# Routing operands in PSUM, late token tiles away from the gather buffer, and the gate computation behind the first split tokens

## The chip, the cores and the metric

The kernel runs on one core of one Trainium2 chip. The metric is the device time of one execution in microseconds (us): the median of three runs of the kernel before is 753.27 us (752.43 to 753.68). A core has five engines that run their own instruction streams: TensorE (PE, products and transposes), VectorE (DVE), ScalarE (ACT), GpSimd (POOL) and SyncE (SP, which starts most transfers). Operands lie in the on-chip memory SBUF; products are written to PSUM, from which DVE and ACT can read and to which they can write.

## The reference

Three layers follow each other on 2304 tokens of 512 numbers (4 batches x 576 positions, 8 heads x 64):

```
kv  = einsum('bhsd,bhse->bhde', k, v)            # attention without softmax
out = einsum('bhsd,bhde->bhse', q, kv)
x   = out / sqrt(mean(out*out) + 1e-6) * g_norm  # norm per token and head

xn, en = x / (|x| + 1e-6), emb / (|emb| + 1e-6)
logits = xn @ en.T / tau                         # 8 experts
expert_idx = argmax(logits);  gate = softmax(logits)[expert_idx]
out[mask]  = gate * (relu(x[mask] @ w1[e]) @ w2[e])   # w1 512x1024, w2 1024x512

h   = x @ w_in;  g = softplus(h)                 # 512 -> 2048
out = g @ w_out                                  # 2048 -> 512
```

## The kernel before

The program has three stages. The head (to about 100 us) computes attention, the norm and the routing, for 18 tiles of 128 tokens. From then on PE works on the experts, one after the other by size ("rank" 0 is the largest), with weights split into two parts of lower precision (wh and wl, as the tokens are into xh and xl), so that one product becomes three (L856 to L858). Then comes the last layer.

In the head, a tile goes through these steps: PE forms the attention output o; ACT squares it (sq, L367) and copies it (cp, L374); DVE sums the squares (ss, L377); for a pair of tiles ACT takes a logarithm and an exponential (rs, L381 and L382) and DVE does a Newton step of three instructions (L151 to L155), which gives rinv; DVE multiplies the logit columns by it (lt, L389) and sums them (lg, L397); POOL multiplies the whole tile by rinv (xa, L403), which a DMA writes to xd in DRAM; and DVE or POOL multiplies xa by g_norm (xo, L416), whose squared norm ACT takes (nn, L419, into ssx). Only the gate needs that norm, the choice of the expert does not.

The tokens are routed in three groups of 6 tiles. For a group DVE finds the best expert (top1, L432 to L442: mx, eq, vm, oh_all), PE counts slots (L451 to L456), DVE forms code, ci, pm and the one-hot tables sel and chk in `early` (L459 to L472), tgb_all (L480), and PE sums them into a token table (L489). DVE counts tokens per expert (acc, L503). After the last group, ranks() sorts the experts by their count (key, cmp, rank, perm, pe, rk_e, L515 to L533) and indices() writes rk_idx (L539 to L547), the rows of xd that each expert wants.

What runs when in the head is decided by a list scheduler: each step has engines, a cost and its predecessors, and the step that can start first with the longest path behind it is issued next; an xo may go to POOL or DVE. Tiles of memory lie in pools: the tile xgt of gathered tokens lies where a head pool was, over xa tiles that were allocated at its start.

Behind the head the code is in written order (L1234 and below). gather() starts POOL's indirect DMAs from xd by rk_idx (L1046), load_w brings weights into st, split_rank makes wh on ACT (CAST, L862) and wl on the named engine (st minus wh, L864); first_transposes turns the gathered tokens on PE (L1076), then ACT makes xh (L1080) and DVE xl (L1084). gates() takes the norm of all tokens (inv_norm: n_x, n_r, L161 to L176), zt = logits minus their maximum (L732), times the norm (L734), exponential on ACT (L736), sum and reciprocal (L739 to L743), then splits the gate in three parts gp (cast and subtract, L747 to L751); each goes into a table tgb (L762), and PE sums these with 18 small products (L766), which stand in PE's program behind the first 36 products of expert 0.

Of the kernel before, what the change touches and what calls it, by code (L numbers as in the profile page):

```python
# [25 lines left out]
def attention_moe_mlp(tc, q, k, v, g_norm, emb, tau, w1, w2, w_in, w_out, out, caps=CAPS):  # L26
# [107 lines left out]
    chk_all = early[:, 64 * NT:76 * NT].bitcast(BF16).rearrange("p (t n) -> p t n", n=3 * E)  # L134
    gate_row, ga_row, rf_row = (early[:, 76 * NT + 384 * i:76 * NT + 384 * i + 384] for i in range(3))
# [13 lines left out]
    def newton(out_, x, r0, r2, half=-0.5):  # L149

        nc.vector.tensor_tensor(out=r2, in0=r0, in1=r0, op=ALU.mult)  # L151
# [34 lines left out]
    with ExitStack() as hs:  # L186
# [147 lines left out]
        xa_t = {i: tp.tile([128, DM], F32, name=f"xa{i}") for i in [*range(7, NT), *range(7)]}  # L334
        xo_t = [tp.tile([128, DM], F32, name=f"xo{i}") for i in range(NXO)]
        ss_t, r0_t, r2_t, rinv_t = ([tp.tile([128, 2, H], F32, name=f"{nm}{i}") for i in range(NSS)] for nm in ("ss", "r0", "r2", "rinv"))
# [77 lines left out]

        def st_xo(t, eng):
            {"G": nc.gpsimd, "D": nc.vector}[eng].tensor_tensor(out=xo_t[t % NXO], in0=xa_t[t], in1=g_rep.rearrange("p h d -> p (h d)"), op=ALU.mult)  # L416

        def st_n(t):
            nc.scalar.activation(out=junk, in_=xo_t[t % NXO], func=AF.Square, accum_out=ssx[:, t:t + 1])  # L419
# [25 lines left out]
        def slots(g):  # L445
# [19 lines left out]
            pm = tp.tile([128, 2, T], I32, name=f"pm{g}")  # L465
# [13 lines left out]
            for u in range(2):  # L479
                nc.vector.tensor_tensor(out=tgb_all[:, u, a:z, :], in0=chk, in1=tok[:, u, a:z].unsqueeze(2).to_broadcast([128, T, 3 * E]), op=ALU.mult)  # L480
                yield

        def tokens(g):
# [7 lines left out]
            if g:  # L491
                nc.vector.tensor_tensor(out=tab, in0=p, in1=tab, op=ALU.add)
            else:
                nc.vector.tensor_copy(tab, p)
# [903 lines left out]
```

## Time and profile before

| | |
|---|---|
| median of 3 runs | 753.27 us (752.43 to 753.68) |
| profiled execution | 752.81 us |
| its span in the profile | 751.0 us |
| mean granted clock of PE | 0.988 of full speed |
| busy: PE, DVE, ACT, POOL | 716.1, 521.9, 408.0, 257.3 us |

The profile is one execution. Times in the rows are microseconds from the start of the span. [...] PE is nearly full from about 100 us to the end; the head is what leaves it waiting.

### The profile page before, as it was taken

Reading aid. Unit: us, or ns where it says so; the run is one execution under the profiler, and the core shown is the slowest. Engines: PE = TensorE matmul, PEld = TensorE weight load, DVE = VectorE, ACT = ScalarE, POOL = GpSimd, SP = SyncE. Lnnn points to the kernel's source line nnn. Section 1 sums busy time; section 2 is a strip of 40 time slices with the busy share of each in tenths; the row PEclk is TensorE's granted clock in tenths of the full one; section 3 lists DMA queues with packets and bytes.
Section 4 is the critical chain, followed back from the end, with each engine's and each line's share of the span. In section 5 each row is a group of like instructions: output and inputs, shape, how many; then the busy total and the mean of one; then the engine's idle time right before and its main releaser. Section 6 shows DMA issues by size and latency. Waiting matters only on the chain.

```text
span 751.0 us, 11433 instructions
## 1 busy us (share of the span) xinstructions
PE 716.1 (95%) x4180; PEld 623.9 (83%) x4180; DVE 521.9 (69%) x944; ACT 408.0 (54%) x753; POOL 257.3 (34%) x190
## 2 busy tenths in 40 slices
PE   9999489999999999998999999999999999999996
PEld 5878279989999999997888878888788878888895
DVE  4588995988688788897787755656555656556564
ACT  2658467646556566554665544445444454345554
POOL 4223456776786877672463020000100020000201
PEclk9999789999999999999999999999999999999999
DMA  9994389898888989831221010000100010000100
GB/s 239 277 265 149 123 277 351 261 324 253 286 280 272 318 282 299 299 96 40 74 84 30 0 57 1 0 1 1 56 1 1 0 43 15 1 1 0 57 1 32
DMA packets 71073, 96.67 MB, mean 129 GB/s; under 512 B 13012, under 2 KB 45804, under 8 KB 71010
## 3 DMA queue, kind: packets, MB, share of 16 engines
q1 hardware_dynamic: 67490, 86.02, 37.3%
q0 software_dynamic: 3344, 9.80, 3.6%
q8 instruction: 35, 0.57, 0.3%
q14 instruction: 28, 0.23, 0.1%
q10 hardware_dynamic: 176, 0.05, 0.0%
HBM read 78.01 MB, written 17.84 MB: 128 GB/s over the span
## 4 chain that ended last, share of the span: by engine, by line
issue 44%; PE 38%; DVE 8%; DMA 4%; ACT 2%; POOL 1%; SPq 1%; ACTq 0%; DVEq 0%; POOLq 0%
PE acc_t L856 9%; PE acc_t L857 9%; PE acc_t L858 9%; DMA out_dram<-orow,idx 2%; PE tp_t L1063 1%; PE misc L301 1%; DMA vr<-in_v_dram 1%; PE tp_t L857 1%; PE tp_t L858 1%; PE tp_t L856 1%; PE acc_t L967 1%; PE acc_t L966 1%; PE acc_t L965 1%; POOL out_dram L972 1%; DVE xs L874 1%
## 5 line engine op out<-in xcount | busy, mean ns | idle before, releaser
L864 POOL TENSOR_TENSOR wl<-st,wh 128x1024 fp32r<-128x1024 f32 x66 | 158.9, 2410 | 71.2 <-ACT wh L862 64.2
L972 POOL DMA_INDIRECT out_dram<-orow,idx x18 | 18.6, 1035 | 324.6 <-ACT orow L971 321.9
L930 ACT ACTIVATE e<-tp_t 128x512 f32<-128x512 f32 (+1 forms) x77 | 42.8, 556 | 131.8 <-PE tp_t L858 131.7
L932 DVE TENSOR_SCALAR u<-e 128x512 f32<-128x512 f32 (+1 forms) x78 | 31.1, 399 | 116.7 <-ACT e L931 116.6
L862 ACT CAST wh<-st 128x1024 fp32r<-128x1024 f32 x72 | 75.2, 1047 | 47.5 <-POOL wl L864 19.7
L856 PE MATMUL acc_t<-hh,wh 128*128 128x368 f32 (+7 forms) x256 | 81.2, 317 | 1.2 <-DVE hl L1213 1.2
L856 PE MATMUL acc_t<-xh,wh 128*128 128x368 f32 (+7 forms) x256 | 79.4, 310 | 0.4 <-ACT x L1230 0.3
L857 PE MATMUL acc_t<-xl,wh 128*128 128x368 f32 (+7 forms) x256 | 79.0, 309 | 0.0
L858 PE MATMUL acc_t<-xh,wl 128*128 128x368 f32 (+7 forms) x256 | 78.9, 308 | 0.0
L858 PE MATMUL acc_t<-hh,wl 128*128 128x368 f32 (+7 forms) x256 | 78.0, 305 | 0.0
L857 PE MATMUL acc_t<-hl,wh 128*128 128x368 f32 (+7 forms) x256 | 78.0, 305 | 0.0
L949 DVE TENSOR_TENSOR gl<-u,gh 128x512 fp32r<-128x512 f32 (+1 forms) x78 | 58.0, 743 | 17.8 <-ACT gh L947 17.8
L938 ACT ACTIVATE u<-u 128x512 f32<-128x512 f32 (+1 forms) x78 | 46.1, 591 | 43.7 <-DVE e L934 43.7
L965 PE MATMUL acc_t<-wh,gh 128*128 128x512 f32 x144 | 56.6, 393 | 5.9 <-ACT gh L947 5.9
L857 PE MATMUL tp_t<-xs,wh 128*128 128x512 f32 (+1 forms) x160 | 59.0, 369 | 0.6 <-DVE xs L874 0.6
L858 PE MATMUL tp_t<-xs,wl 128*128 128x512 f32 (+1 forms) x160 | 58.8, 368 | 0.0
L856 PE MATMUL tp_t<-xs,wh 128*128 128x512 f32 (+1 forms) x160 | 58.8, 368 | 0.0
L967 PE MATMUL acc_t<-wh,gl 128*128 128x512 f32 x144 | 56.5, 392 | 1.3 <-DVE gl L949 1.3
L858 PE MATMUL tp_t<-xs,wl_b 128*128 128x512 f32 (+1 forms) x156 | 57.7, 370 | 0.0
L857 PE MATMUL tp_t<-xs,wh_b 128*128 128x512 f32 (+1 forms) x156 | 57.7, 370 | 0.0
L856 PE MATMUL tp_t<-xs,wh_b 128*128 128x512 f32 (+1 forms) x156 | 57.7, 370 | 0.0
L965 PE MATMUL acc_t<-wh_b,gh 128*128 128x512 f32 x144 | 56.2, 390 | 0.1
(254 smaller groups left out, 1812.0 us busy)
## 6 DMA issues: line engine op xcount, KB each, us to landing
st<-in_moe_w_dram SPq DMA_DIRECT2D x64, 512.0 KB
raw<-in_moe_w_in_dram SPq DMA_DIRECT2D x16, 512.0 KB
raw<-in_moe_w_out_dram SPq DMA_DIRECT2D x16, 512.0 KB
wd<-pre_p SPq DMA_DIRECT2D x32, 256.0 KB
q<-in_q_dram SPq DMA_DIRECT2D x8, 512.0 KB
xd<-xa SPq DMA_DIRECT2D x16, 256.0 KB
st<-wd SPq DMA_DIRECT2D x8, 512.0 KB
raw<-wd SPq DMA_DIRECT2D x8, 512.0 KB
```

What stands on the lines that cost most here:

```text
L856: nc.tensor.matmul(ps_, wh, xh, start=start, stop=False)
L857: nc.tensor.matmul(ps_, wh, xl, start=False, stop=False)
L858: nc.tensor.matmul(ps_, wl, xh, start=False, stop=stop)
L862: nc.scalar.copy(h, raw)
L864: eng.tensor_tensor(out=l, in0=raw, in1=h.bitcast(F32), op=ALU.subtract)
L930: nc.scalar.activation(out=e, in_=h, func=AF.Abs)
L932: nc.vector.tensor_scalar(out=u, in0=e, scalar1=1.0, scalar2=None, op0=ALU.add)
L938: nc.scalar.activation(out=u, in_=u, func=AF.Ln)
L949: nc.vector.tensor_tensor(out=gl, in0=u, in1=gh.bitcast(F32), op=ALU.subtract)
L965: nc.tensor.matmul(mt[b][t_], gh[:, cs_], wh[:, f % 2, :], start=f == 0, stop=False)
L967: nc.tensor.matmul(mt[b][t_], gl[:, cs_], wh[:, f % 2, :], start=False, stop=f == NF - 1)
L972: nc.gpsimd.indirect_dma_start(out=rows_out[i], out_offset=bass.IndirectOffsetOnAxis(ap=idx2[:, i:i + 1], axis=0), in_=o, in_offset=None)
```

## The change

It has three parts. First, the xa of tiles 13 to 17 are allocated ahead of the others, so that the gathered tokens of the first expert lie over xa of tiles 0 to 3. The xo of tiles 10 to 12 are given to POOL, behind its last xa, and those of 13 to 17 to DVE, behind the indices; the last three are kept in `early`. Second, operands of the routing of groups 1 and 2 (mx, eq, pm, key, rank, copies of io8 and tok, the table's last sum) and of the last three Newton steps lie in the PSUM tile misc; key is computed twice, and rs of the late pairs has a second exponential, so that one copy lies in SBUF and one in PSUM. Third, behind the head: zt is formed ahead of the offsets, wl of the first weight piece goes to DVE and of the second to POOL, and gates() stands as a whole behind the transposes and the second weight piece, with the norms of tiles 15 to 17 just ahead of it.

```diff
+    NX0, NX1, NX2 = NT - 8, NT - 5, NT - 3
+    late_xo = [early[:, 76 * NT + 1152 + DM * i:76 * NT + 1152 + DM * i + DM] for i in range(NT - NX2)]
...
-        xa_t = {i: tp.tile([128, DM], F32, name=f"xa{i}") for i in [*range(7, NT), *range(7)]}
+        xa_t = {i: tp.tile([128, DM], F32, name=f"xa{i}") for i in [*range(NX1, NT), *range(NX1)]}
...
-            r0 = r0_t[p % NSS]
+            r0 = r0_t[(p % NSS, "late") if p >= NP1 else p % NSS]
             nc.scalar.activation(out=r0, in_=ss_t[p % NSS], func=AF.Ln)
+            if p >= NP1:
+                nc.scalar.activation(out=r0_t[p % NSS], in_=r0, func=AF.Exp, scale=-0.5, bias=eps)
             nc.scalar.activation(out=r0, in_=r0, func=AF.Exp, scale=-0.5, bias=eps)
...
-            yield from newton(rinv_t[i], ss_t[i], r0_t[i], r2_t[i], -0.5 / D)
+            u = (i, "late") if p >= NP1 else i
+            yield from newton(rinv_t[i], ss_t[i], r0_t[i], r2_t[u], -0.5 / D, r0_t[u])
...
+        def in_misc(*shape, dt=F32):
+            n = int(np.prod(shape))
+            m_at[0] += n
+            tl = misc_t[:, m_at[0] - n:m_at[0]]
+            tl = tl if dt == F32 else tl.bitcast(dt)
+            return tl if len(shape) == 1 else tl.rearrange("p (a b) -> p a b", b=shape[1])
+        NP1 = NT // 2 - 3
+        for i in range(NP1, NT // 2):
+            r0_t[i % NSS, "late"], r2_t[i % NSS, "late"] = in_misc(2, H), in_misc(2, H)
+        def xo_place(t):
+            return late_xo[t - NX2] if t >= NX2 else xo_t[t % NXO]
...
+        tab_l, key, rank_l, io8_l = in_misc(E, 3), in_misc(E), in_misc(E), in_misc(E)
+        tok_l = in_misc(2, TG)
+        mx_l, eq_l = {g: in_misc(TG) for g in range(1, NG)}, in_misc(TG, E)
+        pm_l = in_misc(2, TG, dt=I32)
...
-            mx = mx_all[:, a:z]
+            mx = mx_l[g][:, 0:T] if g else mx_all[:, a:z]
...
-            eq = tp.tile([128, T, E], F32, name=f"eq{g}")
+            eq = eq_l[:, 0:T, :] if g else tp.tile([128, T, E], F32, name=f"eq{g}")
...
-            cnt = misc_t[:, 0:E]
+            cnt = qp_t[1][:, 0, 0:E]
...
-            key = tp.tile([128, E], F32, name="key")
-            nc.vector.scalar_tensor_tensor(out=key, in0=cnt, scalar=float(E), in1=first, op0=ALU.mult, op1=ALU.add)
+            key_s = tp.tile([128, E], F32, name="key")
+            for k_ in (key, key_s):
+                nc.vector.scalar_tensor_tensor(out=k_, in0=cnt, scalar=float(E), in1=first, op0=ALU.mult, op1=ALU.add)
...
+        def st_late():
+            nc.vector.tensor_copy(io8_l, io8)
+            nc.vector.tensor_copy(tok_l, tok[:, :, groups[-1][0]:NT])
...
+                for u in range(NX1, NT):
+                    step(("xo", u), "D", 560, lambda u=u: st_xo(u, "D"), ("idx", 1), ("nn", u - NXO))
+                    if u < NX2:
+                        step(("nn", u), "A", 613, lambda u=u: st_n(u), ("xo", u))
...
-                    step(("xo", u), "GD", (1225, 560), lambda eng, u=u: st_xo(u, eng), ("xa", u), ("nn", u - NXO))
-                    step(("nn", u), "A", 613, lambda u=u: st_n(u), ("xo", u))
+                    if u < NX0:
+                        step(("xo", u), "GD", (1225, 560), lambda eng, u=u: st_xo(u, eng), ("xa", u), ("nn", u - NXO))
+                        step(("nn", u), "A", 613, lambda u=u: st_n(u), ("xo", u))
...
+                if t == NT - 1:
+                    for u in range(NX0, NX1):
+                        step(("xo", u), "G", 1225, lambda u=u: st_xo(u, "G"), ("xa", NT - 1), ("nn", u - NXO))
+                        step(("nn", u), "A", 613, lambda u=u: st_n(u), ("xo", u))
...
             rn = yield from inv_norm(const, ssx, [128, NT], "n")
-            zt = const.tile([128, NT, E], F32, name="zt")
-            nc.vector.tensor_tensor(out=zt, in0=lg_all, in1=mx_all.unsqueeze(2).to_broadcast([128, NT, E]), op=ALU.subtract)
-            yield
             nc.vector.tensor_tensor(out=zt, in0=zt, in1=rn.unsqueeze(2).to_broadcast([128, NT, E]), op=ALU.mult)
             yield
...
+        zt = const.tile([128, NT, E], F32, name="zt")
+        for g, (a, z) in enumerate(groups):
+            mx = mx_l[g][:, 0:z - a] if g else mx_all[:, a:z]
+            nc.vector.tensor_tensor(out=zt[:, a:z, :], in0=lg_all[:, a:z, :], in1=mx.unsqueeze(2).to_broadcast([128, z - a, E]), op=ALU.subtract)
...
-    gts = gates()
-    for _ in range(5):
-        next(gts)
+    split_rank(0, 0, nc.vector)
+    load_w(1, 0)
     fill(tp_tile(), 18)
-    split_rank(0, 0, nc.gpsimd)
-    load_w(1, 0)
     next(pre)
-    for _ in range(5):
-        next(gts)
     first_transposes()
-    split_rank(0, 1, nc.vector)
+    split_rank(0, 1, nc.gpsimd)
     load_w(1, 1)
-    for _ in gts:
+    for u in range(NX2, NT):
+        nc.scalar.activation(out=late_xo[u - NX2], in_=late_xo[u - NX2], func=AF.Square, accum_out=ssx[:, u:u + 1])
+    for _ in gates():
         pass
     split_rank(0, 2, nc.gpsimd)
     load_w(1, 2)
```

In the same way the other operands named above are replaced by their places in misc (tab by tab_l, rank by rank_l, tok by tok_l in the last group).

The next rows are POOL's program from its last xa to the first weights: xa are token tiles, xo those times g_norm, xgt the gathered tokens. Before:

```order
L403 TENSOR_TENSOR xa_278<-oc_268,rinv_307 128x512
L403 TENSOR_TENSOR xa_279<-oc_269,rinv_308 128x512
L403 TENSOR_TENSOR xa_280<-oc_269,rinv_308 128x512
L1046 DMA xgt<-xd,rk_idx 128x512 x2
L1046 DMA xgt<-xd,rk_idx 112x512
L864 TENSOR_TENSOR wl_1186<-st_1130,wh_1184 128x1024
L864 TENSOR_TENSOR wl_1263<-st_1144,wh_1261 128x1024
```

and after the change:

```order
L408 TENSOR_TENSOR xa_273<-oc_269,rinv_308 128x512
L408 TENSOR_TENSOR xa_274<-oc_269,rinv_308 128x512
L438 TENSOR_TENSOR xo_289<-xa_285,g_rep 128x512
L438 TENSOR_TENSOR xo_290<-xa_286,g_rep 128x512
L438 TENSOR_TENSOR xo_291<-xa_287,g_rep 128x512
L1089 DMA xgt<-xd,rk_idx 128x512 x2
L1089 DMA xgt<-xd,rk_idx 112x512
L907 TENSOR_TENSOR wl_1234<-st_1143,wh_1232 128x1024
L907 TENSOR_TENSOR wl_1266<-st_1146,wh_1264 128x1024
```

Three xo stand between the last xa and the gathers, and the first wl product is that of the second weight piece.

ACT's program from its last norm before the expert weights (junk, ssx) to the third weight piece (wh); n_r is the inverse norm, zt the exponential of the gates. Before:

```order
L419 ACTIVATE junk,ssx<-xo_296 128x512
L164 ACTIVATE n_r_1158<-n_x 128x18
L165 ACTIVATE n_r_1158<-n_r_1158 128x18
L862 CAST wh_1184<-st_1130 128x1024
L1080 ACTIVATE xh<-acc_t,gcol 128x256 x3
L1080 ACTIVATE xh<-acc_t,gcol 128x112 x2
L1080 ACTIVATE xh<-acc_t,gcol 128x256
L1080 ACTIVATE xh<-tp_t,gcol 128x112 x2
L862 CAST wh_1245<-st_1141 128x1024
L736 ACTIVATE zt<-zt 128x144
L862 CAST wh_1261<-st_1144 128x1024
```

and after the change:

```order
L441 ACTIVATE junk,ssx<-xo_291 128x512
L905 CAST wh_1158<-st_1132 128x1024
L1123 ACTIVATE xh<-acc_t,gcol 128x256 x3
L1123 ACTIVATE xh<-acc_t,gcol 128x112 x2
L1123 ACTIVATE xh<-acc_t,gcol 128x256
L1123 ACTIVATE xh<-tp_t,gcol 128x112 x2
L905 CAST wh_1232<-st_1143 128x1024
L1293 ACTIVATE early,ssx<-early 128x512 x3
L166 ACTIVATE n_r_1243<-n_x 128x18
L167 ACTIVATE n_r_1243<-n_r_1243 128x18
L775 ACTIVATE zt<-zt 128x144
L905 CAST wh_1264<-st_1146 128x1024
```

Three norms (junk is not used there, the square goes back into `early`), n_r and zt stand between the second and the third weight piece.

DVE's program from the sum of all norms (n_x) on, xl being the lower part of the gathered tokens. Before:

```order
L161 TENSOR_SCALAR n_x<-ssx 128x18
L151 TENSOR_TENSOR n_r_1161<-n_r_1158 128x18
L153 SCALAR_TENSOR_TENSOR n_r_1161<-n_r_1161,n_x 128x18
L155 SCALAR_TENSOR_TENSOR n_r_1158<-n_r_1161,n_r_1158 128x18
L169 TENSOR_TENSOR n_r_1158<-n_r_1158,n_x 128x18
L171 TENSOR_SCALAR n_r_1158<-n_r_1158 128x18
L176 RECIPROCAL n_r_1158<-n_r_1158 128x18
L732 TENSOR_TENSOR zt<-lg_all,mx_all 128x144
L734 TENSOR_TENSOR zt<-zt,n_r_1158 128x144
L1084 SCALAR_TENSOR_TENSOR xl<-acc_t,gcol,xh 128x256 x2
L1084 SCALAR_TENSOR_TENSOR xl<-acc_t,gcol,xh 128x112
L1084 SCALAR_TENSOR_TENSOR xl<-acc_t,gcol,xh 128x256
```

and after the change, with the last xl first:

```order
L1127 SCALAR_TENSOR_TENSOR xl<-tp_t,gcol,xh 128x112 x2
L163 TENSOR_SCALAR n_x<-ssx 128x18
L153 TENSOR_TENSOR n_r_1246<-n_r_1243 128x18
L155 SCALAR_TENSOR_TENSOR n_r_1246<-n_r_1246,n_x 128x18
L157 SCALAR_TENSOR_TENSOR n_r_1243<-n_r_1246,n_r_1243 128x18
L171 TENSOR_TENSOR n_r_1243<-n_r_1243,n_x 128x18
L173 TENSOR_SCALAR n_r_1243<-n_r_1243 128x18
L178 RECIPROCAL n_r_1243<-n_r_1243 128x18
L773 TENSOR_TENSOR zt<-zt,n_r_1243 128x144
L778 TENSOR_REDUCE gate_all<-zt 128x18
L780 TENSOR_SCALAR gate_all<-gate_all 128x18
L782 RECIPROCAL gate_all<-gate_all 128x18
```

The norm and zt were ahead of the xl and are behind them, followed without a break by the sum of the gates.

## Rows read from the trace of the kernel before

**Rows 1.** The page, part 1: busy time of each engine, share of the span, instructions.
```profile
PE 716.1 (95%) x4180; PEld 623.9 (83%) x4180; DVE 521.9 (69%) x944; ACT 408.0 (54%) x753; POOL 257.3 (34%) x190
```

**Rows 2.** The chain of waits, 80 to 111 us: start, us, what.
```profile
100.13 0.65 PE acc_t L856
...
104.11 0.31 PE acc_t L858
...
107.19 0.17 PE acc_t L858
...
108.87 0.72 PE tp_t L766 x18
```

**Rows 3.** Timeline of DVE, 69 to 90.5: start, us, engine, line, operation, out<-in.
```profile
70.95 1.07 DVE L442 TENSOR_TENSOR oh_all<-eq,vm 128x48 bf16<-128x48 f32 x1
...
80.02 0.69 DVE L377 TENSOR_REDUCE ss<-sqb 128x8 f32<-128x520 f32 x1
...
80.70 1.43 DVE L416 TENSOR_TENSOR xo<-xa,g_rep 128x512 f32<-128x512 f32 x1
...
83.96 0.97 DVE L437 TENSOR_TENSOR eq<-eq,first 128x48 f32<-128x48 f32 x1
...
85.19 0.21 DVE L442 TENSOR_TENSOR oh_all<-eq,vm 128x48 bf16<-128x48 f32 x1
...
86.11 0.21 DVE L459 TENSOR_TENSOR code<-rt,oh_all 128x48 f32<-128x48 f32 x1 [0.44 <-PE rt L456]
...
90.02 0.35 DVE L547 TENSOR_REDUCE rk_idx<-pt 128x24 int32<-128x192 f32 x1
```

**Rows 4.** Timeline of POOL, 69 to 110; in brackets idle time and releaser.
```profile
70.69 1.27 POOL L416 TENSOR_TENSOR xo<-xa,g_rep 128x512 f32<-128x512 f32 x1
...
82.78 2.08 POOL L403 TENSOR_TENSOR xa<-oc,rinv 128x512 f32<-128x512 f32 x2 [1.19 <-DVE rinv L155]
92.47 1.34 POOL L1046 DMA_INDIRECT xgt<-xd,rk_idx  x1 [7.61 <-DVE xo L416]
...
104.34 2.40 POOL L864 TENSOR_TENSOR wl<-st,wh 128x1024 fp32r<-128x1024 f32 x1 [5.35 <-ACT wh L862]
```

**Rows 5.** Timeline of DVE, 90 to 110 us.
```profile
94.84 0.23 DVE L161 TENSOR_SCALAR n_x<-ssx 128x18 f32<-128x18 f32 x1
...
96.67 0.27 DVE L176 RECIPROCAL n_r<-n_r 128x18 f32<-128x18 f32 x1
...
103.18 0.30 DVE L739 TENSOR_REDUCE gate_all<-zt 128x18 f32<-128x144 f32 x1
...
104.44 2.33 DVE L747 CAST gp<-left 128x18 bf16<-128x18 f32 x1
...
107.11 1.69 DVE L762 TENSOR_TENSOR tgb<-early,gp 128x432 bf16<-128x432 bf16 x3
```

**Rows 6.** Timeline of ACT, 74 to 105 us.
```profile
77.88 0.58 ACT L367 ACTIVATE sqb<-o 128x512 f32<-128x512 f32 x1
...
80.98 0.31 ACT L382 ACTIVATE r<-r,eps 128x16 f32<-128x16 f32 x1
...
94.08 0.63 ACT L419 ACTIVATE junk<-xo 128x512 f32<-128x512 f32 x1
...
100.83 1.07 ACT L862 CAST wh<-st 128x1024 fp32r<-128x1024 f32 x1
101.77 0.36 ACT L736 ACTIVATE zt<-zt 128x144 f32<-128x144 f32 x1
```

**Rows 7.** Two windows: bounds, length, busy by engine, granted clock, DMA share, GB/s.
```profile
81.36:91.60 10.24, 3.69 (x27) 1.74 (x27) 9.24 (x34) 1.26 (x3) 2.31 (x3) 0.50 0.28 105
98.43:105.26 6.83, 6.13 (x20) 5.54 (x21) 6.62 (x17) 4.96 (x12) 1.48 (x2) 0.50 0.69 198
```

**Rows 8.** Timeline of PE, 76 to 101 us.
```profile
85.45 0.20 PE L451 MATMUL rt<-oh_all,upper 128*128 128x48 bf16 x1 [5.50 <-DVE oh_all L442]
...
96.34 0.63 PE L1076 MATMUL acc_t<-ident,xgt 128*128 128x128 f32 x4 [1.95 <-DMA xgt<-xd,rk_idx]
```

More of the change, by code (lines that the diff above doesn't have):

```diff
@@ L147, in attention_moe_mlp, with newton @@
     nc.scalar.preload_act_table_set("natural_log_exp_and_others")
-    def newton(out_, x, r0, r2, half=-0.5):
-        nc.vector.tensor_tensor(out=r2, in0=r0, in1=r0, op=ALU.mult)
+    def newton(out_, x, r0, r2, half=-0.5, r0b=None):
+        nc.vector.tensor_tensor(out=r2, in0=r0 if r0b is None else r0b, in1=r0, op=ALU.mult)
         yield
@@ L332, in attention_moe_mlp @@
         oc_t = [tp.tile([128, 2, 4, 144], F32, name=f"oc{i}") for i in range(NOC)]
[L334 removed]
+        xa_t = {i: tp.tile([128, DM], F32, name=f"xa{i}") for i in [*range(NX1, NT), *range(NX1)]}
         xo_t = [tp.tile([128, DM], F32, name=f"xo{i}") for i in range(NXO)]
[L336 removed]
+        ss_t, r0_t, r2_t, rinv_t = ({i: tp.tile([128, 2, H], F32, name=f"{nm}{i}") for i in range(NSS)} for nm in ("ss", "r0", "r2", "rinv"))
         lt_t = [tp.tile([128, 2, H, E], F32, name=f"lt{i}") for i in range(2)]
@@ L464, in slots @@
             yield
-            pm = tp.tile([128, 2, T], I32, name=f"pm{g}")
+            pm = pm_l[:, :, 0:T] if g else tp.tile([128, 2, T], I32, name=f"pm{g}")
             nc.vector.tensor_scalar(out=pm[:, 0, :], in0=ci, scalar1=127, scalar2=None, op0=ALU.bitwise_and)
@@ L479, in slots @@
             for u in range(2):
-                nc.vector.tensor_tensor(out=tgb_all[:, u, a:z, :], in0=chk, in1=tok[:, u, a:z].unsqueeze(2).to_broadcast([128, T, 3 * E]), op=ALU.mult)
+                nc.vector.tensor_tensor(out=tgb_all[:, u, a:z, :], in0=chk, in1=(tok_l[:, u, 0:T] if g == NG - 1 else tok[:, u, a:z]).unsqueeze(2).to_broadcast([128, T, 3 * E]), op=ALU.mult)
                 yield
@@ L491, in tokens @@
             if g:
-                nc.vector.tensor_tensor(out=tab, in0=p, in1=tab, op=ALU.add)
+                nc.vector.tensor_tensor(out=tab_l if g == NG - 1 else tab, in0=p, in1=tab, op=ALU.add)
             else:
@@ L603, in route @@
             last_ = g == NG - 1
+            if last_:
+                step(("late",), "D", 160, st_late, ("fin", B - 1, 5), ("top", g - 1, 4))
             gen_ = top1(g)
             for i in range(5):
-                step(("top", g, i), "D", 119, lambda g_=gen_: next(g_), *([("lg", p) for p in range(a // 2, z // 2)] if i == 0 else [("top", g, i - 1)]))
+                step(("top", g, i), "D", 119, lambda g_=gen_: next(g_), *([("lg", p) for p in range(a // 2, z // 2)] + ([("fin", B - 1, 5)] if g else []) + ([("late",)] if last_ else []) if i == 0 else [("top", g, i - 1)]))
             oh = ("top", g, 4)
@@ L642, in attention_moe_mlp @@
             if t % 2:
-                step(("rs", p), "A", 460, lambda p=p: st_rs(p), ("ss", t - 1), ("ss", t), ("n", p - NSS, 2))
+                step(("rs", p), "A", 460, lambda p=p: st_rs(p), ("ss", t - 1), ("ss", t), ("n", p - NSS, 2), *([("fin", B - 1, 5)] if p >= NP1 else []))
                 gen_ = st_newton(p)
@@ L705, in offsets @@
             below = const.tile([128, E, E], F32, name="below")
-            nc.vector.tensor_tensor(out=below, in0=rank.unsqueeze(1).to_broadcast([128, E, E]), in1=io8.unsqueeze(2).to_broadcast([128, E, E]), op=ALU.is_lt)
+            nc.vector.tensor_tensor(out=below, in0=rank_l.unsqueeze(1).to_broadcast([128, E, E]), in1=io8.unsqueeze(2).to_broadcast([128, E, E]), op=ALU.is_lt)
             yield
```

16 lines of the change are left out of this document (8 added, 8 removed).

## The prediction

> **What bounds the kernel now.** I read the page first: TensorE (PE) is busy for 95% of the span [rows 1], so a change in the head of the program can only move the time by moving the moment from which PE runs without a pause, or by opening a pause later. Then the chain of waits between 80 and 111 us: it runs through the routing of the last tokens on VectorE (DVE), the gathered tokens, the first product of expert 0 at 100.13 us, and from there through PE alone; the 18 small products of the gate table stand at 108.87 us between two ordinary products, with no wait before them [rows 2]. So every microsecond by which the product after that table comes earlier or later is a microsecond of the kernel. The reader is to fix three times. T = 90.37 us, the end of the reduce that writes the token indices (90.02 + 0.35) [rows 3]; M = 100.13, the first expert product, which is T + 9.76; G = 108.87, the gate table, which is T + 18.50 [rows 2]. PE takes 8.74 us from M to G.
>
> The timelines by engine give what fills these stretches. On DVE, small instructions are held while GpSimd (POOL) multiplies: oh_all takes 1.07 us at 70.95 and 0.21 at 85.19, and eq, of the same shape, 0.97 at 83.96 [rows 3]; they end when POOL's products of 70.69 and 82.78 end [rows 4]. Those held have all their operands in SBUF. Two more of this kind, a newton step and an xo, are held between 77 and 82 us. The gathers start at 92.47, T + 2.10, released by a DVE xo [rows 4]. The gate chain is the other long one: n_x, the reciprocal, zt and its exponential, then the three parts gp with a cast of 2.33 us beside POOL's wl product of 104.34, and the three tgb products that end at 108.80 (107.11 + 1.69) [rows 4 to 6]. That is 0.07 us before the table starts: the gates are just in time already.
>
> **The change part by part.** *Routing up to the indices.* The operands that were held go to PSUM. An instruction with one operand there costs no more: code, with rt in PSUM, takes 0.21 us and oh_all, of the same shape, 0.21 [rows 3]. [...] Before the last norm DVE loses two xo, one of them the 1.43 us of 80.70 [rows 3], and three holds of 0.76 to 0.86, and gains two copies of about 0.2. But not all of that is on the path. The last ss reduce (80.02) [rows 3] is followed by ScalarE's (ACT) logarithm and, at 80.98, an exponential of 0.31 [rows 6], and only then newton starts, which the xo of 80.70 held to its end at 82.1. Without that xo, and with one more exponential (0.25 from start to start), it starts near 81.5: 0.55 us earlier. If the ss reduce moves up too, to the end of its square at 78.46 (77.88 + 0.58) [rows 6], 1.56 more are to be had; some of it goes to new holds (lt and the first tgb of the second group now lie beside POOL's xa). I take 0.9, from 0.55 to 2.1. After it, eq loses its hold (0.76), while acc, with both operands in SBUF, now lies beside the first of the three xo that go to POOL behind the last xa: a hold of up to 0.97 by the row of eq; I take 0.57, what is left of that product by then. The shared PSUM tile makes pm, key, rank and tgb follow one another, each with about 0.1 us of handover where pairs now overlap, and key is made twice: I take 0.5 from 0 to 1. That stretch comes out 0.3 longer. T' = T - 0.6; the bounds are T - 0.2 and T - 2.9 (0.55 + 1.56 + 0.76 and nothing lost).
>
> *Gather.* xgt no longer lies over the late xa, so the gathers wait for the indices and not for a third xo behind them. POOL's three xo (1.27 each [rows 4]) start behind its last xa, at 84.86, and end by 88.7, before T'. The first gather starts at T' + 0.3, against T + 2.10: 1.8 us sooner. From gather to first product I keep 7.66 (100.13 - 92.47), so M' = T' + 7.96. The weights st, of which two pieces load from 90.4 on, share the queues with it more than before, so a loss of 0 to 0.5 is possible (the wait of 0.3 us between two gathers is the nearest size) and I take none. PE's fill, which ended 1.95 us before the first transposes of 96.34 [rows 8], ends just before the first transposes then, and doesn't hold them. M' - M = -2.4.
>
> *Gates.* This part goes the other way. Norms 15 to 17 now stand on ACT behind the cast wh_1, which itself stands behind the xh of the gathered tokens: it starts at M + 0.70 (100.83) and lasts 1.07 [rows 6], so it ends at T' + 9.73. The three norms at 0.75 each (the last one of before starts at 94.08 and n_x at 94.84) [rows 5, 6] end at T' + 11.9. Then n_x to the end of the reciprocal, 2.10 (94.84 to 96.94), zt by n_r 0.3 (as the reduce of the same size at 103.18) [rows 5] and the exponential 0.36 [rows 6]: it ends at e = T' + 14.7. Before, it ended at 102.12 (101.77 + 0.36), T + 11.75. From the reduce of gate_all to the end of tgb it was 5.62 us (103.18 to 108.80) [rows 5], and the hold of the cast comes again: the cast wh_2 on ACT now stands behind that exponential, ends at e + 1.0, and lets POOL's 2.4 us product wl start just as DVE comes to its second gp, at e + 1.27. So tgb is there at e + 5.6, and the table starts at G' = T' + 20.4, against T + 18.5. With T' that is 1.3 us later than before. PE reaches the table at M' + 8.74 = T' + 16.7 and stands for 3.7 us, the whole of what the gather gave and more. If PE's clock should be full before it, PE stands for longer and G' stays. What is queued behind the table on PE is the rest of expert 0; nobody else is needed for it, since wl of the next columns is done at e + 3.4.
>
> *Clock.* A pause of PE has a price behind it in this trace. [...] The bounds are 0 and 3.6 (the longer, 10.24). I take 2.1.
>
> *Sum.* -0.6 (indices) and +1.9 (gates behind the indices) and +2.1 (clock) = +3.4 on the profiled execution's 752.81 us: 756.2. The median of the runs, 753.27, is 0.46 above it, so 756.7. After G' PE is full, as it is for 95% of the span [rows 1], and nothing gives the time back.
>
> **The rivals.** *The clock stays* (0.18). PE paused for 1.95 us before 96.34, between the two stretches at 0.50, and the clock did not fall until 98.43 [rows 7, 8]. Then only +1.3 is left: 754.6. *POOL stays out of DVE's way* (0.17, the other side). If the operands in PSUM free DVE for good, T' comes near T - 2.0; and if POOL's wl starts only after the third gp, as it would where the weights for wh_2 land late, the 2.3 us of hold in the gate chain go. Then G' = T' + 18.1 = T + 16.1, PE stands only 1.4 us, the clock holds, and the kernel takes 750.8. It decides from the point at which the table starts before 107.3, 1.5 us sooner than now. Against it: the new order puts that cast behind the exponential, when the weights have long landed. *The indices gain much, the gates as I have them* (0.12): T' = T - 2.0, G' = G - 0.1, and the clock still costs 2.1: 755.3. *The gather loses against the weights* (0.08): M', and with it wh_1 and the norms, come 0.5 to 1 us later: 757.5. That the table doesn't wait at all for the late norms is excluded by the order: n_x needs all of ssx.
>
> **How the numbers follow.** My forecast has 0.45, with a range of its own of 754.9 to 758.4 from the bounds of the clock and the indices. A measurement can tell about 0.2% from no change, 1.5 us: below 751.8 is faster, above 754.8 slower. Faster is the rival of that sign, 0.17. Same takes half of the rival on the clock, half of that on the indices and a little of the forecast's edge: 0.18. Slower is the rest, 0.65. The range goes from 751.2 to 758.5: below it lies most of the faster case, above it the long fall of the clock.
>
> **What would show it.** The first gather should follow the indices by 0.3 us, and the first expert product come near 97.7 us. PE should pause before the gate table, near 106.5 us if cold, for 3 to 4 us, released by DVE's tgb; the second or third step of the gp chain should last over 2 us beside POOL's wl; ACT's three late norms should stand between wh_1 and wh_2. The granted clock should read 0.50 over the products behind the table. acc should be held beside POOL's xo. I am wrong if PE finds the table's operands ready, or if the pause is there and short; wrong in size if the clock reads 1.00 behind it.

## The result

The changed kernel is slower: 758.6 us, the median of five runs (756.65 to 759.95), against 753.08 of the kernel before (752.43 to 753.68), a ratio of 1.0065 with a 95% interval of 1.0045 to 1.0085. In a second series of ten runs, on the chip of the last experiments, it took 757.19 (756.2 to 757.79) against 752.96, 1.0050 (1.0037 to 1.0063). The ratios take in all runs and need not be those of the medians. The two series put the cost at 5.5 and at 4.2 us, where 3.4 were forecast.

The profiled execution of the changed kernel took 759.01 us with a span of 757.2. PE is busy for 1.6 us more than before [rows 1], while the span is 6.2 us longer, so most of the time is waiting and not work:

```profile
PE 717.7 (95%) x4180; PEld 625.2 (83%) x4180; DVE 517.7 (68%) x947; ACT 408.5 (54%) x756; POOL 260.3 (34%) x192
```

The timeline of PE shows where. In the columns stand the start, the length, the line and the operation, and in brackets the idle time before it and what ended it:

```profile
97.25 1.32 PE L1119 MATMUL acc_t<-ident,xgt 128*128 128x128 f32 x8 [1.25 <-DMA xgt<-xd,rk_idx]
...
99.79 0.44 PE L899 MATMUL acc_t<-xh,wh 128*128 128x368 f32 x1 [0.32 <-DVE xl L1127]
...
106.19 0.33 PE L901 MATMUL acc_t<-xh,wl 128*128 128x368 f32 x1
112.47 1.24 PE L809 MATMUL tp_t<-tgb,early 128*128 128x72 bf16 x18 [5.96 <-DVE tgb L805]
...
113.97 0.51 PE L900 MATMUL acc_t<-xl,wh 128*128 128x368 f32 x1
```

The first expert product (L899) comes at 99.79 us, 0.34 sooner than the 100.13 of [rows 2]. PE has done its first 36 products at 106.52 and then stands for 5.96 us before the gate table (L809), which waits for DVE's tgb. In the kernel before, the table followed at 108.87 without a wait. Behind it the products are 0.31 us apart again.

DVE's timeline has the way to that tgb:

```profile
86.01 0.67 DVE L529 TENSOR_TENSOR acc<-acc,red 128x8 bf16<-128x8 bf16 x1
...
90.92 0.35 DVE L573 TENSOR_REDUCE rk_idx<-pt 128x24 int32<-128x192 f32 x1
...
103.64 0.64 DVE L163 TENSOR_SCALAR n_x<-ssx 128x18 f32<-128x18 f32 x1 [2.03 <-ACT early L1293]
...
106.88 0.30 DVE L778 TENSOR_REDUCE gate_all<-zt 128x18 f32<-128x144 f32 x1 [0.39 <-ACT zt L775]
...
107.94 2.29 DVE L790 TENSOR_TENSOR left<-gate_all,gp 128x18 f32<-128x18 f32 x1
...
110.78 1.64 DVE L805 TENSOR_TENSOR tgb<-early,gp 128x432 bf16<-128x432 bf16 x3
```

POOL's timeline has what stands beside it:

```profile
85.39 3.71 POOL L438 TENSOR_TENSOR xo<-xa,g_rep 128x512 f32<-128x512 f32 x3
91.56 1.34 POOL L1089 DMA_INDIRECT xgt<-xd,rk_idx  x1 [2.46 <-DVE rk_idx L573]
...
101.85 2.40 POOL L907 TENSOR_TENSOR wl<-st,wh 128x1024 fp32r<-128x1024 f32 x1 [6.10 <-ACT wh L905]
107.86 2.35 POOL L907 TENSOR_TENSOR wl<-st,wh 128x1024 fp32r<-128x1024 f32 x1 [3.61 <-ACT wh L905]
```

acc is held beside POOL's first xo, 0.67 us for an addition of eight columns; the first gather follows the indices by 0.29 us (91.27 to 91.56) and no longer by 2.1 [rows 4]. But n_x, the start of the gate chain, stands at 103.64 and not at 94.84 [rows 5]; it is held to the end of POOL's wl of the second piece, and left, in the chain's middle, takes 2.29 us beside wl of the third. On ACT the late norms (read from and written to early) stand behind wh_1, and the exponential ends at 106.84:

```profile
100.67 1.09 ACT L905 CAST wh<-st 128x1024 fp32r<-128x1024 f32 x1
101.61 0.69 ACT L1293 ACTIVATE early<-early 128x512 f32<-128x512 f32 x1
...
106.52 0.32 ACT L775 ACTIVATE zt<-zt 128x144 f32<-128x144 f32 x1 [1.74 <-DVE zt L773]
```

The windows show the granted clock (third number from the end; the second number is PE's busy time):

```profile
46.00:50.00 4.00, 4.00 (x26) 3.71 (x27) 1.76 (x7) 2.94 (x7) 0.00 (x0) 0.57 1.13 269
99.50:106.50 7.00, 6.71 (x36) 6.00 (x37) 4.18 (x15) 4.55 (x14) 2.40 (x1) 1.00 0.73 246
111.00:117.60 6.60, 5.12 (x31) 5.12 (x31) 6.17 (x9) 0.84 (x2) 2.74 (x3) 0.50 1.07 364
```

It is full while PE works through the first 36 products, unlike in [rows 7], and at half from 111.0 to 117.6, behind the long pause. The row at 46 us is not the change's doing: PE pauses there for 1.55 us at the same place in both kernels, and in this one execution the clock fell behind it, which moved everything after it by about 1.4 us. A second profile of the same kernel, from the other series, has the clock at 1.00 there and is the one to set against the kernel before. It took 757.79 us with a span of 755.9. From DVE's timeline:

```profile
84.62 0.67 DVE L529 TENSOR_TENSOR acc<-acc,red 128x8 bf16<-128x8 bf16 x1
...
89.52 0.35 DVE L573 TENSOR_REDUCE rk_idx<-pt 128x24 int32<-128x192 f32 x1
...
102.37 0.64 DVE L163 TENSOR_SCALAR n_x<-ssx 128x18 f32<-128x18 f32 x1 [2.03 <-ACT early L1293]
...
106.66 2.30 DVE L790 TENSOR_TENSOR left<-gate_all,gp 128x18 f32<-128x18 f32 x1
```

And from PE's:

```profile
95.84 0.63 PE L1119 MATMUL acc_t<-ident,xgt 128*128 128x128 f32 x4 [1.13 <-DMA xgt<-xd,rk_idx]
...
98.51 0.44 PE L899 MATMUL acc_t<-xh,wh 128*128 128x368 f32 x1 [0.59 <-DVE xl L1127]
...
111.20 1.24 PE L809 MATMUL tp_t<-tgb,early 128*128 128x72 bf16 x18 [5.96 <-DVE tgb L805]
112.25 0.66 PE L899 MATMUL acc_t<-xh,wh 128*128 128x368 f32 x1
```

The indices end at 89.87 us, 0.5 sooner than before; the first expert product comes 1.6 sooner, the gate table 2.35 later, and PE stands for the same 5.96 us. From about 130 us on every instruction runs 4.8 us behind the kernel before, and so it stays to the end (4.9 in the span).

### The profile page after: what moved, and what is told of

It reads as the page before. It is cut to its first block, busy times and chain, and to the rows that moved or that the text cites. A ratio compares the mean times of both kernels' runs of the same rounds, so it can differ in the third digit from the quotient of the medians.

```text
span 757.2 us, 11445 instructions
## 1 busy us (share of the span) xinstructions
PE 717.7 (95%) x4180; PEld 625.2 (83%) x4180; DVE 517.7 (68%) x947; ACT 408.5 (54%) x756; POOL 260.3 (34%) x192
## 4 chain that ended last, share of the span: by engine, by line
issue 44%; PE 39%; DVE 8%; ACT 3%; DMA 3%; POOL 2%; SPq 0%; ACTq 0%; DVEq 0%; POOLq 0%
PE acc_t L899 9%; PE acc_t L900 8%; PE acc_t L901 8%; DMA out_dram<-orow,idx 2%; PE tp_t L1106 1%; PE misc L303 1%; PE tp_t L900 1%; PE tp_t L901 1%; PE tp_t L899 1%; PE acc_t L1010 1%; PE acc_t L1008 1%; PE acc_t L1009 1%; PE o L362 1%; POOL out_dram L1015 1%; DVE xs L917 1%
## 5 line engine op out<-in xcount | busy, mean ns | idle before, releaser
L899 PE MATMUL acc_t<-hh,wh 128*128 128x368 f32 (+7 forms) x256 | 81.2, 317 | 1.3 <-DVE hl L1256 1.2
L899 PE MATMUL acc_t<-xh,wh 128*128 128x368 f32 (+7 forms) x256 | 79.4, 310 | 0.7 <-ACT x L1273 0.3
L899 PE MATMUL tp_t<-xs,wh 128*128 128x512 f32 (+1 forms) x160 | 58.8, 368 | 0.0
L899 PE MATMUL tp_t<-xs,wh_b 128*128 128x512 f32 (+1 forms) x156 | 57.7, 370 | 0.0
```

What stands on the lines that cost most here:

```text
L899: nc.tensor.matmul(ps_, wh, xh, start=start, stop=False)
```

## The experiments

**Only the place of the tiles** (kernel before):

```diff
-        xa_t = {i: ... for i in [*range(7, NT), *range(7)]}
+        xa_t = {i: ... for i in [*range(NT - 5, NT), *range(NT - 5)]}
```

> The kernel before with one line changed: the xa of tiles 13 to 17 are allocated first, so the gather buffer lies over xa of tiles 0 to 3; nothing else moves. Theory (the gate table sets the end, and it was just in time before): the first gather starts 0.3 us behind the indices instead of 2.1, the first expert product comes 1.8 us earlier, the table does not, PE stands 1.5 to 2 us before it, and the time stays at 753 us (755 if the clock falls behind the pause). Rival (the gather is what the path needs): the 1.8 us reach the end, 751.3 us.

Measured: 752.92 us against 752.93, 1.0007 (0.9991 to 1.0022). The time is as the theory said, but not for its reason: the first product does not come earlier. POOL issues the first gather at 90.57 instead of 92.47, and the first transposes stand at 96.28 instead of 96.34 [rows 8]:

```profile
90.57 1.34 POOL L1046 DMA_INDIRECT xgt<-xd,rk_idx  x1 [5.81 <-DVE rk_idx L547]
```

```profile
96.28 0.63 PE L1076 MATMUL acc_t<-ident,xgt 128*128 128x128 f32 x4 [1.73 <-DMA xgt<-xd,rk_idx]
...
100.05 0.64 PE L856 MATMUL acc_t<-xh,wh 128*128 128x368 f32 x1 [1.65 <-ACT xh L1080]
```

The bytes per queue tell why the tokens are no earlier. In this kernel, from 91.0 to 94.5 us (queue and kind, packets, MB, share of the 16 engines) only the weights' queue moves anything:

```profile
q1 hardware_dynamic: 979, 0.99, 88.6%
```

From 94.5 to 99.5 the gather's queue, q0, moves all of its 0.75 MB:

```profile
q0 software_dynamic: 240, 0.75, 41.8%
q1 hardware_dynamic: 93, 0.08, 4.7%
```

The kernel before has no packet of q0 before 94.5 either, and the same 240 afterwards. SP orders two weight pieces (st, 1.05 MB) just ahead of the gather, at 90.3, and in both kernels the gathered tokens come only behind them, whether POOL asks at 90.57 or at 92.47. That holds for the first tokens. The last transposes end 1.6 us sooner than before (98.40 against 100.03), and the first product is still at 100.05. The bracket names ACT's xh, but DVE is late there too: its gate step zt is held beside POOL's first wl product, and xl begins only behind it, at 99.42, against 99.50 before. In both kernels the first product follows that start by 0.63 us:

```profile
96.69 2.31 DVE L732 TENSOR_TENSOR zt<-lg_all,mx_all 128x144 f32<-128x144 f32 x1
```

So an earlier gather alone is worth nothing here, for two reasons: the weights ahead of it, and DVE behind it. Whether xh or xl let the product go, the trace does not settle.

**The table later** (changed kernel; the scales that need its result move along):

```diff
-            if m in (2, 3):
+            if m in (5, 6):
                 next(gq)
-            if m in (4, 7):
+            if m in (6, 7):
                 next(gr)
```

> The changed kernel with the gate table's 18 products behind the sixth block of products of expert 0 instead of the third (and what follows from them later as well). Theory (the late gates and the clock behind the pause are the whole loss): PE no longer stands 6 us, only about 1.3 us where the third weight piece's wl is ready at 110.2 us; no stretch at half clock behind it; 750.5 to 752.5 us, under the kernel before. Rival (the head's routing or the gather is what got slower): 757 us or more as the changed kernel.

Measured: 760.32 us, 1.0097 (1.0080 to 1.0114): a miss. PE does not wait for the table any more, but twice for hl (the lower part of the hidden layer, as xl is of the tokens), which DVE makes behind its wl products, and once for the gate's rows, which this edit brought close behind the table. With a wait of 0.47 us for POOL's wl at 109.49 that is 7.05 us in all:

```profile
113.30 0.43 PE L899 MATMUL acc_t<-xh,wh 128*128 128x368 f32 x1 [1.86 <-DVE hl L1258]
...
117.60 0.44 PE L899 MATMUL acc_t<-xh,wh 128*128 128x368 f32 x1 [1.33 <-DVE hl L1258]
...
125.30 0.54 PE L1165 MATMUL tp_t<-ident,early 128*128 128x128 f32 x3 [3.39 <-DVE early L1160]
```

```profile
113.16 3.93 DVE L907 TENSOR_TENSOR wl<-st,wh 128x1024 fp32r<-128x1024 f32 x1
```

One wl product of DVE takes 3.93 us there, beside POOL's of 113.60 to 116.00, where the one of 111.58 takes 1.22. So this edit does not take the loss away: DVE's queue behind the late chain is the next thing that PE waits for, and moving the table does not shorten it. As the edit makes a new wait of its own, of 3.39 us, it does not settle what the pause alone is worth.

**The pause filled** (changed kernel):

```diff
+            if m == 2:
+                fill(tp_tile(), 24)
             if m in (2, 3):
                 next(gq)
```

> The changed kernel with 24 products of no use (0.216 us each, 5.2 us) put on PE just before the gate table, so that PE works through most of its pause. Theory (the pause lowers the clock, which costs 14 products at 0.14 us behind the table): the granted clock stays 1.00 from 106 to 118 us, the table stands where it stood, and the time falls by 2.0 us against the changed kernel, to 756.6 us. Rival (the clock's fall has another cause, or the pause alone costs all): the clock falls all the same and the time stays at 758.6 us.

Measured: 755.74 us, 1.0044 (1.0023 to 1.0066), 1.45 us under the changed kernel's 757.19 in medians; in the profile it stands at a span of 754.0 against 755.9. The table is as late as ever (PE starts it at 111.73; the tokens, and all behind them, came 0.5 us later in this execution than in the second profile of the changed kernel), but the clock stays:

```profile
106.50:111.70 5.20, 4.45 (x21) 1.91 (x20) 4.99 (x11) 4.55 (x8) 4.17 (x3) 1.00 1.06 382
111.70:117.60 5.90, 5.87 (x50) 5.87 (x50) 5.87 (x9) 2.42 (x4) 3.10 (x3) 1.00 1.08 357
```

So the half clock behind the pause is caused by PE's standing. It costs 1.45 us in medians and 1.9 in spans, and about 2.4 when the 0.5 us of the late tokens are allowed for: 14 products at 0.14 us, and 0.5 for the table's own products, which take 0.74 us here and 1.24 there.

**The third wl off POOL** (changed kernel):

```diff
-    split_rank(0, 2, nc.gpsimd)
+    next(gq)
+    split_rank(0, 2, nc.vector)
     load_w(1, 2)
     for c in range(3):
         gather(1, c)
-    next(gq)
```

> The changed kernel with the wl product of the third weight piece moved from POOL to DVE, behind the three tgb products, so that POOL does not work beside the gate chain; POOL's three gathers for the second expert come earlier by that. Theory (the hold of 2.29 us in the gate chain is POOL's product): the step left takes 0.2 us, the table starts 2.3 us earlier, PE stands 3.7 us, and the time falls by 2.3 us, to 756.3 us. Rival (DVE is held by something else there, or the gathers beside it hold it as well): the step stays over 1 us and the time within 0.7 us of 758.6.

Measured: 756.69 us (753.68 to 761.61, five runs), 1.0065 (1.0034 to 1.0097). The step behaves as the theory says: left takes 0.18 us and the table starts at 109.54 instead of 111.20. PE stands for 1.52 us:

```profile
107.12 0.18 DVE L790 TENSOR_TENSOR left<-gate_all,gp 128x18 f32<-128x18 f32 x1
```

```profile
109.54 0.74 PE L809 MATMUL tp_t<-tgb,early 128*128 128x72 bf16 x18 [1.52 <-DVE tgb L805]
```

Most of that shorter pause is not the edit's: in this execution the clock read 0.57 from 98 to 106 us, so PE took some 2 us longer over its first 36 products. What the edit is worth in time stays open, as these five runs lie 8 us apart, with mean granted clocks from 0.974 to 0.987, and the profiled one is the fastest of them.

**One weight piece ahead of the gather** (changed kernel):

```diff
-    for i in range(2):
+    for i in range(1):
         load_w(0, i)
     nc.sync.dma_start(out=seen, in_=xgs[0][0:1, 2, 0:1])
-    for i in range(2, 8):
+    for i in range(1, 8):
```

> The changed kernel with one weight piece (0.5 MB) instead of two ordered ahead of the first gather; the second follows the gather. In the runs so far the gather's packets begin only when the 1.09 MB of both pieces are through, whenever POOL issued it. Theory (the weights ahead of it in the transfer queues set when the gathered tokens land): the packets begin about 1.5 us earlier, the first transposes come at 94.5 to 95 us instead of 96.2, the first expert product near 97.7, the table (behind wh_1, which is behind xh) about 1.3 us earlier; 757 us against 758.6. Rival (the gather's own latency sets it): transposes stay at 96.2 and the time does not move.

Measured: 759.24 us, 1.0084 (1.0065 to 1.0103), slower than the changed kernel. The transposes came as the theory said, at 94.92 us, and the first product at 98.08. But the second piece, ordered behind the gather, was late, and the cast wh_1, ahead of the norms, started at 101.67, against 99.40 in the changed kernel; the table came at 113.39. SP ordered that piece only at 97.75, behind `seen`, where the changed kernel ordered it at 89.94. PE waits for it as well, 1.84 us at 105.22 for POOL's wl. The weights do hold the gather: with one piece ahead the first transposes follow its order at 90.45 by 4.47 us, right behind PE's fill, where with two it was 5.67 (changed kernel) and 5.71 (place of the tiles). Putting one piece behind it only moves the wait.

```profile
94.92 0.63 PE L1119 MATMUL acc_t<-ident,xgt 128*128 128x128 f32 x4
```

```profile
101.67 1.05 ACT L905 CAST wh<-st 128x1024 fp32r<-128x1024 f32 x1 [2.54 <-issue]
```

```profile
105.22 0.43 PE L901 MATMUL acc_t<-xh,wl 128*128 128x368 f32 x1 [1.84 <-POOL wl L907]
```

The bracket of the cast names no transfer; that it waits for the piece follows from SP's late order.

**Only the PSUM operands** (kernel before, with the second part of the change: in_misc, late rs, st_late, the routing's operands).

```diff
-            mx = mx_all[:, a:z]
+            mx = mx_l[g][:, 0:T] if g else mx_all[:, a:z]
...
+        tab_l, key, rank_l, io8_l = in_misc(E, 3), in_misc(E), in_misc(E), in_misc(E)
```

> The kernel before with the second part of the change alone: routing operands in PSUM, with the late exponential and the copies; token tiles, xo, norms and gates as before. Theory (it shortens the way to the indices by what DVE is no longer held): the indices end 0.4 to 0.9 us earlier, at 89.5 to 90.0, gather, gates and table follow by as much, and the time is 752.2 to 752.6 us. Rival (PSUM operands cost more than the holds they avoid): the indices end at 90.4 or later and the time is 753 us or more.

Measured: 752.54 us, 0.9987 (0.9971 to 1.0004): not to be told from before. The indices end at 89.47, 0.9 sooner, and the table starts at 107.94, as much sooner. PE, with more of its first 36 products at full clock, stands 1.41 us before it:

```profile
107.94 0.74 PE L805 MATMUL tp_t<-tgb,early 128*128 128x72 bf16 x18 [1.41 <-DVE tgb L801]
```

**Only the place of the gates** (kernel before):

```diff
-    gts = gates()
-    for _ in range(5):
-        next(gts)
+    split_rank(0, 0, nc.vector)
+    load_w(1, 0)
     fill(tp_tile(), 18)
...
     first_transposes()
-    split_rank(0, 1, nc.vector)
+    split_rank(0, 1, nc.gpsimd)
     load_w(1, 1)
-    for _ in gts:
+    for _ in gates():
```

> The kernel before with the third part of the change alone: gates() as a whole behind the transposes and the second weight piece, wl of the first piece on DVE, of the second on POOL; norms and tiles as before. Theory (the place of the gate chain is what makes the table late): the exponential of zt ends near 105.5 us instead of 102.1, tgb near 111, PE stands about 2 us before the table, the clock falls behind it; 755 to 757 us. Rival (only the late norms do it): the table is less than 0.5 us late and the time stays at 753 us.

Measured: 757.29 us, 1.0055 (1.0036 to 1.0073): the loss of the whole change, from one part. The chain is held twice by POOL: n_r's first multiplication beside wl of the second piece (101.85 to 104.25), and left beside that of the third (107.31 to 109.66). The table comes at 111.92, near the 111 expected:

```profile
101.52 0.16 DVE L161 TENSOR_SCALAR n_x<-ssx 128x18 f32<-128x18 f32 x1
102.22 2.06 DVE L151 TENSOR_TENSOR n_r<-n_r 128x18 f32<-128x18 f32 x1 [0.54 <-ACT n_r L165]
...
107.39 2.30 DVE L751 TENSOR_TENSOR left<-gate_all,gp 128x18 f32<-128x18 f32 x1
```

```profile
111.92 1.24 PE L766 MATMUL tp_t<-tgb,early 128*128 128x72 bf16 x18 [5.41 <-DVE tgb L762]
```

PE stands for 5.41 us, where 2 were expected. Most of the difference is PE itself: its clock reads 1.00 over the first 36 products, which it has done 6.7 us after the first one and not 8.74.

The norms are early here (n_x could start at 101.52) and the chain is as late as with the late norms. So late norms are not needed for the loss. In the changed kernel they end just before POOL's product does; without them that product would hold the next step of the chain, and how much would be left no run shows. The edit moves two things at once, the gates and the engines that make the first two wl pieces. No run moves one without the other, so how much of the loss is the place and how much POOL's hold of n_r stays open.

**The gates back in their place** (changed kernel, third part undone, all norms ahead of wh_0):

```diff
+                    step(("nn", u), "A", 613, ..., ("xo", u), *[("nn", k) for k in range(NX0, NX1)])
...
+    gts = gates()
+    for _ in range(5):
+        next(gts)
     fill(tp_tile(), 18)
+    split_rank(0, 0, nc.gpsimd)
...
+    for _ in range(4):
+        next(gts)
     first_transposes()
+    split_rank(0, 1, nc.vector)
```

> The changed kernel with its third part undone: gates() split around the transposes as before, wl of the first piece on POOL and of the second on DVE, all norms ahead of the first weight piece with those of tiles 10 to 12 first; tiles and PSUM operands as changed. Theory (the place of the gate chain is the loss, the other two parts cost nothing): tgb ends near 108.0 to 108.5, PE stands 1.5 us or less, 752 to 753 us. Rival (the routing with three xo on POOL, or the late tiles, loses as well): 755 us or more.

Measured: 752.29 us (751.51 to 753.09) against 752.96, 0.9985 (0.9972 to 0.9998). The loss is gone. The kernel is about 0.1% under the one before, about the least that can be told at all. This run undoes the third part and also takes the norms forward, so it shows the two together. PE's wait before the table is half a microsecond:

```profile
98.91 0.64 PE L898 MATMUL acc_t<-xh,wh 128*128 128x368 f32 x1 [1.33 <-DVE xl L1126]
...
107.34 0.74 PE L808 MATMUL tp_t<-tgb,early 128*128 128x72 bf16 x18 [0.51 <-issue]
```

> The changed kernel itself, word for word, on the chip of this study, to set the runs with the filled pause (755.7 us) and with wl on DVE (756.7 us) against. Theory (the clock behind the pause costs 14 products at 0.14 us, the fill took that away): 757.5 to 758.5 us, with the half clock from about 110 to 117 us. Rival (the fill gained nothing and the chip differs): 756 us or less.

This is the second series told of above: 757.19 us, a little under the theory's 757.5 to 758.5 and above the rival's 756. The half clock is there, 0.58 from 111.0 to 117.6 us, where the kernel before has 1.00.

**Three attempts at more.** The first repairs the changed kernel: norms of tiles 10 to 12 first, one weight piece ahead of the gather, POOL away from the gate chain.

```diff
+    split_rank(0, 0, nc.gpsimd)
...
     first_transposes()
+    gts = gates()
+    for _ in range(9):
+        next(gts)
+    split_rank(0, 1, nc.vector)
...
+    next(gq)
+    split_rank(0, 2, nc.vector)
```

> The changed kernel with three repairs: the norms of tiles 10 to 12 ahead of those of 13 to 17 and all of them ahead of the first weight piece, so that n_x needs no norm behind xh; one weight piece ahead of the gather; wl of the first piece on POOL, of the second and third on DVE, the third behind tgb, so that POOL doesn't work beside the gate chain. Theory (late gates, POOL's hold and the weights ahead of the gather are what keeps the gain away): first expert product near 98.2 us, tgb ready by 105 us, no wait at the table, 749.5 to 751.5 us, under the kernel before. Rival (another wait takes the place, DVE's queue of wl products above all): PE stands behind the table for wl or hl and the time is 753 us or more.

Measured: 753.22 us, 1.0000 (0.9990 to 1.0009). The loss is gone and no gain has come, so the rival has the better of it in time. In the profile PE waits 0.66 us for DVE's wl at 108.62, 1.39 before the table and 0.47 for hl at 124.77. But the profiled execution took 757.94 us, 4.7 above the median: its clock fell at 46 us, and by 55 us PE is some 4 us behind the kernel before. Which waits a usual execution has is not shown. The second adds to the kernel with the PSUM operands alone:

```diff
+    next(gq)
+    split_rank(0, 2, nc.vector)
     load_w(1, 2)
     for c in range(3):
         gather(1, c)
+    split_rank(0, 3, nc.gpsimd)
```

> The kernel with routing operands in PSUM (e6_psum) and POOL kept away from the gate chain: wl of the third weight piece on DVE behind tgb, the three gathers of the second expert ahead of wl of the fourth on POOL. Theory (in e6_psum the table, held 2.3 us by POOL's wl, is what PE waits for, 1.41 us): tgb ends near 105.6 us instead of 107.9, PE meets the table without a wait near 106.5, and the time is 750.8 to 751.6 us. Rival (DVE's queue or the weights take the hold's place, as behind the table in e8_best): PE waits for wl or hl within the next blocks and the time stays at 752.5 us.

Measured: 752.79 us, 1.0003 (0.9986 to 1.0019). In the profile PE meets the table without a wait, yet nothing is to be seen in the time. That profile too is of a long execution (756.66 us) whose clock fell at 46 us, so whether a usual one has no wait there is open. The third adds one weight piece ahead of the gather to that, and the others behind its first tile:

```diff
-    nc.sync.dma_start(out=seen, in_=xgs[0][0:1, 2, 0:1])
+    nc.sync.dma_start(out=seen, in_=xgs[0][0:1, 0, 0:1])
```

> As e9_psum_wl, with one weight piece ahead of the gather and the others ordered as soon as its first tile has landed, not its last. Theory (the weights ahead of the gather delay the first product; ordered so, the second piece lands in time, unlike in e5_one_weight): first transposes near 94.3 us, first expert product near 98.0, the second piece landed by 98, table near 105.5, 749.8 to 751 us. Rival (the pieces ordered behind the first tile now delay the second and third tile of the gather, or wh_1 comes late as in e5_one_weight): the time is that of e9_psum_wl or above.

Measured: 753.61 us, 1.0001 (0.9985 to 1.0017). The pieces ordered behind the first tile now hold the third, for which PE waits 2.01 us, and the first product comes at 101.23, as the rival has it.

## Why the prediction was right, and where its sizes were off

Right in its direction and in the cause: the gate chain behind the first split tokens makes the table late, PE stands before it, the clock falls behind the pause. Doing the third part alone brings the loss (757.29 us); undoing it, with the norms taken forward, takes the loss away (752.29); and filling the pause keeps the clock. Within that part, the place of the gates and the exchange of engines for the wl pieces were not told apart. The forecast of 756.7 lies under the 757.2 and 758.6 measured. Its own range of 754.9 to 758.4 holds the first; 758.6 is just above its end and above the 758.5 of the wider range, while the ratio of that series, 1.0065 of 753.27, gives 758.2, inside both. By its own steps, against the profile of the second series:

*Indices.* T' = T - 0.6 was forecast; T - 0.5 it is. The hold of acc came (0.67), as did those of the first and second tgb of the second group (0.64 and 1.15 us), and the four Newton and top1 steps lost theirs. So oh_all, with one operand in PSUM, takes 0.21 us while POOL works beside it (68.42 to 70.51), where it took 1.07 [rows 3]:

```profile
70.04 0.21 DVE L468 TENSOR_TENSOR oh_all<-misc,vm 128x48 bf16<-128x48 f32 x1
```

*Gather.* This step failed. The gather did start at T' + 0.3, but "from gather to first product I keep 7.66" does not hold: it took 8.34 (90.17 to 98.51), and 8.2 to 8.8 in five profiles with this head. Two things changed inside it. From the gather to the first transposes it took 5.67 us where 3.87 were kept, as the weights stand ahead: a loss of 1.8, put at "0 to 0.5" with none taken. From there to the first product it took 2.67 where 3.79 were kept, so 1.1 came back, as the tokens follow one another closer and xl no longer stands behind zt. In the kernel before, the gather was asked for at 92.47 and its packets came at about 94.6, as the weights ended, so it lost little by them. M' - M is -1.6 and not -2.4.

*Gates.* G' = T' + 20.4 was forecast, and T' + 21.3 it is. The exponential ends at T' + 15.7 instead of T' + 14.7: 0.9 by the late tokens (wh_1 stands behind their xh and ends at T' + 10.6 instead of 9.7) and 0.4 by a hold of n_x beside wl of the second piece, which the prediction did not have, less 0.3 for three norms that follow each other by about 0.62 us and not by 0.75. From there to tgb 5.6 us passed, as the 5.62 taken, with left in place of the cast as the held step. That the hold came with the forecast length, but on another step, is partly luck.

*Pause and clock.* PE stands for 5.96 us, where 3.7 were forecast, "longer" if its clock was full before, which it was. The clock was to cost 2.1 us. No run shows that term; in its place the profile shows products of 368 columns 0.31 us apart behind the pause and 0.17 later, 14 of them at 0.14 us more, 2.0. The 18 table products themselves take 1.24 us instead of 0.72, which the sum did not have. The filled pause puts both together at about 2.4 us in spans.

In sum: indices -0.5, gates +2.8, table and clock about +2.4, which gives 4.7 of the 4.8 us. Of the rivals, the one with POOL out of DVE's way did not come, as POOL held n_x, left and acc. The gather that loses against the weights, given 0.08, is what happened, and about as it said: M' came 0.7 us later than forecast and wh_1 0.9, and its 757.5 is nearer to the 757.2 measured than the forecast's 756.7. The range holds both, so the time alone does not tell them apart; the rows of the gather do.

The operands in PSUM cost nothing that these rows show: the kernel with PSUM operands alone ends the indices 0.9 us sooner, and in the second series oh_all, which now reads one of them, takes the 0.21 us that it took at 85.19 [rows 3]. In the same trace n_x, with a single input of 18 columns, which lies in SBUF, takes 0.64 us beside POOL's product, and 0.16 where it starts before POOL does, at 101.52 in the kernel with the gates alone moved.

## What to carry to other kernels

Where two chains meet at one instruction, shortening one of them is worth nothing until the other has been measured. Here the table was just in time before, so a delay of the gates became a loss, and an earlier token alone was no gain. Of an earlier transfer, ask what stands ahead of it in the queues, and not only when it is issued. And a long pause of PE can cost more than its length: behind the one of 5.96 us PE ran at half clock for some 5.4 us, about 2.4 us more. Behind the pauses of 1.41 us (PSUM operands alone) and 1.52 us (third wl off POOL) before the table the clock stayed at 1.00, while the one of 1.55 us at 46 us lowered it in some executions.

## What the runs showed of the hardware

Gathered rows asked for by POOL at 90.57 us moved no byte before 94.5, when 0.99 of the 1.05 MB of weights ordered 0.3 us before them had moved. With half as many weights ahead, the first transposes followed the order by 4.47 us instead of 5.71. How much of such a wait is the gather's own preparation was not told apart.

The clock fell to half behind the same pause of 1.55 us at 46 us in one profile of the changed kernel and not in the other (1.54 us there), which cost the first about 1.4 us. In the profiles of the first two attempts at more it stayed at half until about 56.7 us, and these executions took 4.7 and 3.9 us more than the medians of their kernels. So executions of one program can lie several microseconds apart by this alone.

With one operand in PSUM, DVE's small instructions were not held while POOL worked: eq took 0.97 us in the kernel before and 0.22 in the changed one, oh_all 1.07 and 0.21, and a Newton step 1.01 and 0.17.
